# Attention mixed with a Fourier transform on one core: the first score of a full section ahead of the first product, and a value product that waits for the last exponential

## Chip, core and metric

The kernel runs on one core of one Trainium2 chip. The metric is device time of one execution in microseconds, as the median of several runs. Lower is better. The core's engines are named as in the profile: PE multiplies matrices, PEld is its loading of weights, DVE (vector), ACT (scalar), POOL and SP.

## What is computed

Sequence 2048, width 512, 32 heads of 16. Two branches over the same length are mixed by a gate for each row: a Fourier mixing of `A_x` (two transforms by matrix products, real part) and full softmax attention over the same input.

```python
a = jnp.einsum("bsd,ed->bse", x, dft_hid_re)
b = jnp.einsum("bsd,ed->bse", x, dft_hid_im)
y = jnp.einsum("ts,bse->bte", dft_seq_re, a) - jnp.einsum("ts,bse->bte", dft_seq_im, b)
...
qkv = (x @ wqkv)                      # 32 heads, Dh = 16
p = softmax(einsum("bhqd,bhkd->bhqk", q, k) * scale)
o = jnp.einsum("bhqk,bhkd->bhqd", p, v) @ wo
...
g = _sigmoid((x * gate_w).sum(-1, keepdims=True))
return g * a_branch + (1 - g) * b_branch
```

In the reference both branches read `A_x` (`x = A_x`).

## The kernel before

Everything is laid out by hand: the program text gives each engine its order, and PE's order is written as patterns of slots.

Heads are taken in 16 pairs. For a pair, two kinds of score matmul run over the same queries and keys. `a_tile` (L277) makes a tile `a` of 128 queries by 512 keys (matmul at L283), of which DVE takes the row maximum (L285). `scores` (L751) makes a tile `s` of 128 keys by 512 queries (L764), shifted by the maxima found earlier; ACT takes its exponential into a tile `pt` (L765). A head's operands lie in one half of the partitions, 48 or 50 rows, so a score matmul occupies half of the array's rows. `pv` (L778) multiplies the exponentials by the values: four matmuls of 128 by 17 into the four 32-partition strips of one accumulator `acc` (L786), over 16 key tiles; then ACT copies `acc` out (L790). A unit is one key tile of 512 exponentials for each of two query blocks and two heads; `pt` has four buffers.

In the other half of the array's rows, at the same time, run the products of the Fourier transform over the sequence: `dft` (L480) yields them, `Chain.mm` (L446) issues them (L450). An accumulation chain takes 48 products of full depth; each is split into the two halves of the rows, and they are issued in groups of 16, first all 16 in one half, then the same 16 in the other.

`segment` (L889) issues one such half: a section. `pairs` (L921) sends two sections for each group; 192 sections are "full" (`FULL`, L863). A full section has 16 slots and ends with the value products of two units, eight matmuls. In each slot one product `d` is issued with the one half of the rows, and then one score, `s` or `a`, with the other half; the number in a slot is the PSUM bank that the score goes to. Six banks serve the scores, ACT and DVE give them back. The two patterns are:

```python
FULL = "s2 a3 s4 a1 s5 s2 a0 s3 a4 s1 a5 s2 a0 s3 a4 a1 | |", "a5 s2 a1 s0 a4 s3 a5 s2 s0 a1 a3 s4 s2 s5 a0 a1 | |"
```

The second is used in one of eight, where `acc` has just been finished and ACT has it to copy: 24 sections begin with a maximum's score `a`, 168 with an `s`. The bank of slot 0 in the first pattern, 2, is taken again in slots 5 and 11; slot 13's bank, 3, is that of slot 7; slot 15's bank, 1, that of slot 9.

The first product of a section carries a wait, set by hand (L910): when its chain has begun, for the user (exponential or reduction) of the last score that the section before issued after its last product. In the patterns that is the reduction of `a1`. The chain's bank `d` is a single one: a new chain's first product waits until ACT has read the chain before.

Of the kernel before, what the change touches and what calls it, by code (L numbers as in the profile page):

```python
# [22 lines left out]
NT = S // P  # L23
# [8 lines left out]
def mix_kernel(ctx: ExitStack, tc: tile.TileContext, xa_t, xa, wqkv, w_hid, w_seq, wo, gate_w, out):  # L32
# [5 lines left out]
    nc = tc.nc  # L38
# [59 lines left out]
    acc = psO.tile([P, 512], F32, name="acc")  # L98
# [91 lines left out]
    with tc.tile_pool(name="qk", bufs=1, reuse_waits="tile") as pool:  # L190
# [38 lines left out]
        for tb in range(4):  # L229
# [4 lines left out]
            for c in range(2):  # L234
                if tb == 0 and c == 0:
                    pss = [bank() for _ in range(4)]
                    for kt in range(KT):
                        x = xab[tb][:, :, :, kt * P:(kt + 1) * P]
                        for i, (w, v) in enumerate(((wh, 0), (wl, 0), (wh, 1))):
                            for ct in range(4):  # L240
                                nc.tensor.matmul(pss[ct], w[:, c, kt, ct * P:(ct + 1) * P], x[:, :, v],
                                                 start=kt == 0 and i == 0, stop=kt == KT - 1 and i == 2)
# [15 lines left out]
    vt = main.tile([P, NT, NP, 33], F32, name="vt")  # L258
# [18 lines left out]
    def a_tile(i, h, ps=None, bank=None):  # L277
        p, j = divmod(i, 64)
        qt, kb = divmod(j, 4)
        if ps is None:  # L280
            ps = psA.tile([P, 512], F32, "a", bank)
        r = slice(64 * h, 64 * h + 48)
        nc.tensor.matmul(ps, qs[p % 2][r, qt * P:(qt + 1) * P], ks[p % 2][r, kb * 512:(kb + 1) * 512],  # L283
                         start=True, stop=True)
        user = nc.vector.tensor_reduce(mx[p % 2][:, h, qt, kb:kb + 1], ps, AX.X, ALU.max)  # L285
        hf = j // 32
        a_left[p, hf] = a_left.get((p, hf), 64) - 1
        if not a_left[p, hf]:
            deferred.extend((partial(m_parts, p, hf), partial(m_rows, p, hf)))
        return user  # L290
# [460 lines left out]
    def scores(u, qb, h, bank=(psS, "s"), number=None):  # L751
        p, r = divmod(u, 32)
        hf, kt = divmod(r, 16)
        q0 = hf * 1024 + qb * 512
        if u >= UNITS - 16:

            blk, kt = divmod(kt, 8)
            q0, kt = 1024 + blk * 512, 2 * kt + qb
        if u not in pts:
            pts[u] = work.tile([P, 4, 512], F32, name="pt", bufs=4)  # L760
        pool, name = bank
        ps = pool.tile([P, 512], F32, name=name) if number is None else pool.tile([P, 512], F32, name, number)
        rr = slice(64 * h, 64 * h + 50)
        nc.tensor.matmul(ps, ks[p % 2][rr, kt * P:(kt + 1) * P], qs[p % 2][rr, q0:q0 + 512], start=True, stop=True)  # L764
        return nc.scalar.activation(pts[u][:, 2 * qb + h], ps, AF.Exp, bias=0.0, scale=DH ** -0.5)  # L765

    def pv_last(u):
        blk, k2 = divmod(u - UNITS + 16, 8)
        pt = pts.pop(u)
        for j in range(4):  # L770
            x, h = divmod(j, 2)
            nc.tensor.matmul(acc[32 * j:32 * j + 17], vt[:, 2 * k2 + x, NP - 1, 16 * h:16 * h + 17], pt[:, j],  # L772
                             start=k2 == 0, stop=k2 == 7)
        if blk == 0 and k2 == 7:
            last_pairs.append(LastPair(0, [(psS, "s"), (psA, "a")]))
            last_pairs[0].copy(1)

    def pv(u):  # L778
        if u >= UNITS - 16:
            return pv_last(u)  # L780
        p, r = divmod(u, 32)
        hf, kt = divmod(r, 16)
        pt = pts.pop(u)
        for j in range(4):
            h = j % 2
            nc.tensor.matmul(acc[32 * j:32 * j + 17], vt[:, kt, p, 16 * h:16 * h + 17], pt[:, j],  # L786
                             start=kt == 0, stop=kt == NT - 1)
        if kt == NT - 1:
            oe = work.tile([P, 512], F32, name="oe", bufs=2)
            nc.scalar.copy(oe, acc)  # L790
            for qb in range(2):
                nc.sync.dma_start(o_d[hf][p, :, qb * 512:(qb + 1) * 512], oe[64 * qb:64 * qb + 64])

    def take(gen, n, whole=True):

        got = []
        while len(got) < n:
            x = next(gen, None)
            if x is None:
                break  # L800
            x[0].left -= 1
            got.append((*x, x[0].left == 0))
            if whole and got[-1][4]:
                break
        return got

    def issue(x, half, stop=True):
        chain, st, mv, after, last = x
        i = chain.mm(st, mv, half, last and stop)
        if stop and after:  # L810
            after()
        return i
# [15 lines left out]
    for hf in range(2):  # L828
        for ct in range(4):
            n = 3 if hf and ct == 3 else 4  # L830
# [32 lines left out]
    FULL = "s2 a3 s4 a1 s5 s2 a0 s3 a4 s1 a5 s2 a0 s3 a4 a1 | |", "a5 s2 a1 s0 a4 s3 a5 s2 s0 a1 a3 s4 s2 s5 a0 a1 | |"  # L863
# [10 lines left out]

    streams = [stream(h) for h in range(2)]

    users, valued = [], 0

    def score(kind, h, number=None):
        x = next(streams[h][kind == "a"], None)  # L880
        if x:
            users.append((kind, a_tile(*x, bank=number) if kind == "a" else scores(*x, number=number)))

    def values():
        nonlocal valued
        pv(valued)
        valued += 1

    def segment(pattern, half, ds, stop):  # L889


        nonlocal users
        before, users = users, []
        ds = iter(ds)
        for slot in pattern.split():
            number = None
            if slot[1:].isdigit():
                slot, number = slot[0], int(slot[1])
            if slot == "|":
                values()  # L900
                continue
            if len(slot) == 1:
                x = next(ds, None)
                if x:

                    before = before if x[0].begun else None
                    i = issue(x, half, stop)
                    users = []
                    if before:
                        tc.add_manual_dep(  # L910
                            i.ins, dict(before).get("s", before[0][1]).ins.name,
                            mybir.DependencyInfo(mybir.DependencyClass.Sync, mybir.DependencyReason.DATA))
                        before = None
            if slot != "-":
                score(slot[-1] if slot[0] == "+" else slot[0], 1 - half, number)
            if len(slot) == 2 and slot[0] != "+":
                score(slot[1].lower(), half)
        if deferred:
            deferred.pop(0)()
# [17 lines left out]
    pump(hid, 12)  # L937
    ds = take(hid, 12)
    segment(START[0], 0, ds, False)
    pump(hid, 12)  # L940
    segment(START[1], 1, ds, True)
    values()
    values()
    for patterns, ds in pairs():
        for half in range(2):
            run_plan(valued)
            pattern = FULL[valued % 16 == 0] if patterns is FULL else patterns[half]
            segment(pattern, half, ds, half == 1)
# [14 lines left out]
    for u in range(valued + 2, UNITS, 2):  # L963
# [12 lines left out]
        values()  # L976
    last_pairs[0].products([(psS, "s"), (psA, "a"), (psA, "a"), (psD, "d")], range(4))
    pv(UNITS - 2)
    pv(UNITS - 1)
    last_pair(late)  # L980

# [35 lines left out]
```

## Time and profile before

| | |
|---|---|
| median of 3 runs | 1703.69 us (1703.32 to 1705.98) |
| the profiled execution, in all | 1703.4 us |
| its span | 1701.6 us |
| PE busy | 1693.8 us, 13040 matmuls |
| PE's weight loads busy | 1053.0 us |
| DVE busy | 1352.7 us |
| ACT busy | 1152.2 us |
| POOL busy | 449.7 us |
| granted TensorE clock | 1.0 |
| HBM traffic | 107.73 MB read, 54.52 MB written |

The profile is one execution. A row of the groups names the line of the kernel, the engine, the operation, output and input tiles, shapes and count, then busy time and mean duration, and behind the second bar the idle time just before and what ended it. A row of the timeline has its start and its duration in microseconds, then engine, line and operation; a count above one means that neighbouring rows of one kind were drawn together, from the first one's start to the last one's end. PEld is a load of weights, PE the matmul that uses them. What stands in brackets is the engine's idle time before and the engine and tile that ended it. Matmuls are pipelined and their ends are modelled: a matmul of 512 columns is shown with some 0.39 us, though the next of the same half starts 0.23 us later.

### The profile page before, as it was taken

The page shows a single profiled execution, that of the slowest core. Times are in us where ns is not written, and L with a number is a line of the kernel's source. Part 1 is how long each engine was busy: PE and PEld are TensorE (multiplying, and loading weights), DVE is VectorE, ACT ScalarE, POOL GpSimd, SP SyncE. Part 2 cuts the span into 40 slices and gives each one's busy share as a digit, 9 for nine tenths or more (in the row PEclk, how much of TensorE's full clock was granted, in tenths as well). Part 3 has the DMA queues.
Part 4 walks back from the last instruction along what each step waited for, and adds up shares of the span by engine and source line. Part 5 has one row for each costly group of instructions (what it writes and reads, how often), then busy time and mean ns, then how long its engine had stood idle before and what let it go on. Part 6 is the DMA issues. An engine that isn't in the chain of part 4 may idle for free.

```text
span 1701.6 us, 33689 instructions
## 1 busy us (share of the span) xinstructions
PE 1693.8 (100%) x13040; PEld 1053.0 (62%) x13040; DVE 1352.7 (79%) x2289; ACT 1152.2 (68%) x2266; POOL 449.7 (26%) x554
## 2 busy tenths in 40 slices
PE   9999999999999999999999999999999999999998
PEld 7888755556666666666666666666666666655444
DVE  5439888888888888888888888888888888889854
ACT  5212377777767777667777777776677777678886
POOL 0101121322222333222222343322323343211110
PEclk9999999999999999999999999999999999999999
DMA  9963500314141434314146435224141535352114
GB/s 294 346 144 136 154 8 17 42 38 76 57 77 45 88 97 99 71 39 82 38 94 243 96 107 109 67 60 79 46 86 57 122 106 102 131 183 42 32 34 138
DMA packets 82130, 165.10 MB, mean 97 GB/s; under 512 B 19444, under 2 KB 19682, under 8 KB 78130
## 3 DMA queue, kind: packets, MB, share of 16 engines
q1 hardware_dynamic: 77874, 162.12, 37.1%
q8 instruction: 103, 1.69, 0.4%
q0 software_dynamic: 3808, 0.30, 0.2%
q14 instruction: 57, 0.47, 0.1%
q10 hardware_dynamic: 288, 0.52, 0.1%
HBM read 107.73 MB, written 54.52 MB: 95 GB/s over the span
## 4 chain that ended last, share of the span: by engine, by line
PE 99%; DMA 0%; DVE 0%; ACT 0%; DVEq 0%; issue 0%
PE d L450 37%; PE acc L786 27%; PE a L283 12%; PE s L764 10%; PE s L364 3%; PE s L396 1%; PE d L364 1%; PE acc L772 1%; PE a L107 1%; PE a L106 1%; PE s L107 1%; PE s L106 1%; PE a L105 1%; PE s L105 1%; PE s L450 1%; PE a L450 0%
## 5 line engine op out<-in xcount | busy, mean ns | idle before, releaser
L285 DVE TENSOR_REDUCE mx<-a 128x1 f32<-128x512 f32 x2026 | 1241.0, 682 | 242.6 <-PE a L283 212.8
L765 ACT ACTIVATE pt<-s 128x512 f32<-128x512 f32 x2006 | 1022.6, 620 | 359.4 <-PE s L764 289.9
L764 PE MATMUL s<-qs,ks 50*128 50x512 f32 x2006 | 787.0, 422 | 0.0
L283 PE MATMUL a<-ks,qs 48*128 48x512 f32 x2026 | 744.3, 400 | 0.0
L450 PE MATMUL d<-xab,ch 64*128 64x512 f32 x2016 | 648.0, 396 | 0.0
L786 PE MATMUL acc<-pt,vt 128*17 128x512 f32 x3968 | 484.1, 596 | 0.0
L450 PEld LDWEIGHTS d<-xab,ch 64*128 64x128 f32 x2016 | 365.1, 184 | 124.2 <-DVE mx L285 60.4
L764 PEld LDWEIGHTS s<-qs,ks 50*128 50x128 f32 x2006 | 365.0, 185 | 68.9 <-issue 16.8
L283 PEld LDWEIGHTS a<-ks,qs 48*128 48x128 f32 x2026 | 369.4, 186 | 60.1 <-DVE mx L285 23.9
L450 PE MATMUL d<-xab,cl 64*128 64x512 f32 x1008 | 399.3, 396 | 0.0
L450 PEld LDWEIGHTS d<-xab,cl 64*128 64x128 f32 x1008 | 185.5, 184 | 63.7 <-DVE mx L285 40.8
L434 POOL CAST ch<-craw 128x512 fp32r<-128x512 f32 x126 | 77.2, 612 | 551.2 <-PE a L283 214.2
L786 PEld LDWEIGHTS acc<-pt,vt 128*17 128x17 f32 x3968 | 86.0, 96 | 201.3 <-issue 201.3
L435 POOL TENSOR_TENSOR cl<-craw,ch 128x512 fp32r<-128x512 f32 x126 | 162.1, 1287 | 10.2
L308 POOL DMA_DIRECT2D qs<-mt x119 | 67.0, 568 | 157.7 <-DVE mt L302 155.2
L450 PE MATMUL d<-wre,xab 64*128 64x512 f32 x336 | 90.4, 402 | 0.0
L450 PEld LDWEIGHTS d<-wre,xab 64*128 64x128 f32 x336 | 59.0, 184 | 38.6 <-issue 23.3
L450 PE MATMUL d<-wo_hl,o_hl 64*128 64x512 f32 (+1 forms) x246 | 68.2, 409 | 0.0
L450 PEld LDWEIGHTS d<-wo_hl,o_hl 64*128 64x128 f32 (+1 forms) x246 | 42.2, 184 | 29.3 <-issue 12.2
L101 ACT CAST hl<-s 128x512 fp32r<-128x512 f32 x28 | 16.2, 588 | 58.4 <-PE d L364 25.1
L468 POOL CAST xab<-y 128x512 fp32r<-128x512 f32 x16 | 9.8, 611 | 127.7 <-ACT y L466 99.6
L637 POOL TENSOR_TENSOR yp<-yp,few 128x512 f32<-128x512 f32 x12 | 15.4, 1281 | 105.3 <-ACT few L636 105.2
(167 smaller groups left out, 1000.5 us busy)
## 6 DMA issues: line engine op xcount, KB each, us to landing
craw<-w_seq SPq DMA_DIRECT2D x128, 256.0 KB
qk<-hl SPq DMA_DIRECT2D x32, 512.0 KB
qs<-qk SPq DMA_DIRECT2D x96, 128.0 KB
ks<-qk SPq DMA_DIRECT2D x96, 128.0 KB
b<-hl SPq DMA_DIRECT2D x16, 512.0 KB
xab<-b SPq DMA_DIRECT2D x16, 512.0 KB
o<-oe SPq DMA_DIRECT2D x62, 128.0 KB
oh<-nh SPq DMA_DIRECT2D x12, 512.0 KB
```

Of the source, the lines that this page charges most:

```text
L105: nc.tensor.matmul(ps, sh, mh, start=first, stop=False)
L106: nc.tensor.matmul(ps, sh, ml, start=False, stop=False)
L283: nc.tensor.matmul(ps, qs[p % 2][r, qt * P:(qt + 1) * P], ks[p % 2][r, kb * 512:(kb + 1) * 512], start=True, stop=True)
L285: user = nc.vector.tensor_reduce(mx[p % 2][:, h, qt, kb:kb + 1], ps, AX.X, ALU.max)
L308: (nc.gpsimd if own else nc.sync).dma_start(rows.rearrange("v (q b c) -> v b q c", q=8, b=4)[:, b], mt[hf][32 * b + h:32 * b + 32:2])
L364: i = nc.tensor.matmul(ps, st[r], mv[r], start=not half and not j, stop=half == 1 and j == 11)
L434: nc.gpsimd.tensor_copy(h1, raw)
L435: nc.gpsimd.tensor_tensor(l1, raw, h1.bitcast(F32), ALU.subtract)
L450: i = nc.tensor.matmul(self.ps, st[r], mv[r], start=not self.begun, stop=stop)
L764: nc.tensor.matmul(ps, ks[p % 2][rr, kt * P:(kt + 1) * P], qs[p % 2][rr, q0:q0 + 512], start=True, stop=True)
L765: return nc.scalar.activation(pts[u][:, 2 * qb + h], ps, AF.Exp, bias=0.0, scale=DH ** -0.5)
L786: nc.tensor.matmul(acc[32 * j:32 * j + 17], vt[:, kt, p, 16 * h:16 * h + 17], pt[:, j], start=kt == 0, stop=kt == NT - 1)
```

## The change

Three things, all in the issuing of full sections. `pv` and `values` return the last matmul of the value products, and `score` keeps the latest exponential. At the end of a full section the last matmul of the second unit's value products gets a dependency on the section's last exponential (that of slot 13). And in slot 0 of a pattern whose slots are numbered, which only the full patterns are, the score is issued ahead of the product; in the other slots the product stays ahead. So PE's order at the section's start is score, product, product, score, product, score, where it was product, score, product, score. The product's own wait is kept.

```diff
@@ pv
-            nc.tensor.matmul(acc[32 * j:32 * j + 17], vt[:, kt, p, 16 * h:16 * h + 17], pt[:, j],
-                             start=kt == 0, stop=kt == NT - 1)
+            i = nc.tensor.matmul(acc[32 * j:32 * j + 17], vt[:, kt, p, 16 * h:16 * h + 17], pt[:, j],
+                                 start=kt == 0, stop=kt == NT - 1)
...
+        return i
@@ score, values
-    users, valued = [], 0
+    users, valued, exponential = [], 0, None
...
+            if kind == "s":
+                exponential = users[-1][1]
...
-        pv(valued)
+        i = pv(valued)
         valued += 1
+        return i
@@ segment
-        for slot in pattern.split():
+        for n, slot in enumerate(pattern.split()):
...
             if slot == "|":
-                values()
+                i = values()
+                if n == len(pattern.split()) - 1 and pattern in FULL:
+                    tc.add_manual_dep(i.ins, exponential.ins.name,
+                                      mybir.DependencyInfo(mybir.DependencyClass.Sync, mybir.DependencyReason.DATA))
                 continue
+            if not n and number is not None:
+                score(slot, 1 - half, number)
             if len(slot) == 1:
                 x = next(ds, None)
...
-            if slot != "-":
+            if slot != "-" and (n or number is None):
                 score(slot[-1] if slot[0] == "+" else slot[0], 1 - half, number)
```

DVE's, ACT's, POOL's and SP's instructions and their order are the same in both programs; on PE the 192 first scores move by one place. Which instruction of PE announces its end to the other engines is settled when the program is built: an instruction's count is carried by the next one behind it, so long as that one waits for nothing.

More of the change, by code (lines that the diff above doesn't have):

```diff
@@ L875, in mix_kernel @@
     streams = [stream(h) for h in range(2)]
-    users, valued = [], 0
+    users, valued, exponential = [], 0, None
     def score(kind, h, number=None):
+        nonlocal exponential
         x = next(streams[h][kind == "a"], None)
```

## The prediction

> **What bounds the kernel now.** I read the page first: PE is busy throughout, and the chain that ended last stays on it.
>
> ```profile
> span 1701.6 us, 33689 instructions
> PE d L450 37%; PE acc L786 27%; PE a L283 12%; PE s L764 10%; PE s L364 3%; PE s L396 1%; PE d L364 1%; PE acc L772 1%; PE a L107 1%; PE a L106 1%; PE s L107 1%; PE s L106 1%; PE a L105 1%; PE s L105 1%; PE s L450 1%; PE a L450 0%
> L285 DVE TENSOR_REDUCE mx<-a 128x1 f32<-128x512 f32 x2026 | 1241.0, 682 | 242.6 <-PE a L283 212.8
> L765 ACT ACTIVATE pt<-s 128x512 f32<-128x512 f32 x2006 | 1022.6, 620 | 359.4 <-PE s L764 289.9
> L786 PE MATMUL acc<-pt,vt 128*17 128x512 f32 x3968 | 484.1, 596 | 0.0
> ```
>
> A busy PE hides waits inside its matmuls, so I went to the timeline of one full section, in order of time (start, duration). Times below are differences of starts.
>
> ```profile
> 598.12 1.04 PE L786 MATMUL acc<-pt,vt 128*17 128x512 f32 x8
> ...
> 599.09 0.18 PEld L450 LDWEIGHTS d<-xab,cl 64*128 64x128 f32 x1 [0.85 <-DVE mx L285]
> 599.10 0.50 PE L450 MATMUL d<-xab,cl 64*128 64x512 f32 x1
> ...
> 599.10 0.49 PE L764 MATMUL s<-qs,ks 50*128 50x512 f32 x1
> ...
> 599.43 0.39 PE L450 MATMUL d<-xab,ch 64*128 64x512 f32 x1
> ...
> 599.66 0.60 ACT L765 ACTIVATE pt<-s 128x512 f32<-128x512 f32 x1 [1.91 <-PE s L764]
> ...
> 600.31 0.18 PEld L764 LDWEIGHTS s<-qs,ks 50*128 50x128 f32 x1
> ...
> 601.59 1.12 ACT L765 ACTIVATE pt<-s 128x512 f32<-128x512 f32 x2
> ...
> 602.66 0.39 PE L450 MATMUL d<-xab,cl 64*128 64x512 f32 x1
> 602.76 0.18 PEld L283 LDWEIGHTS a<-ks,qs 48*128 48x128 f32 x1
> ...
> 602.84 0.42 PE L283 MATMUL a<-ks,qs 48*128 48x512 f32 x1
> 603.18 0.62 PE L786 MATMUL acc<-pt,vt 128*17 128x512 f32 x4
> ```
>
> The reader is to see a loop through ACT. The value products' block ends at 599.16 (598.12 + 1.04); product and first score start at 599.10. The first exponential starts 0.56 after that score and ends at 600.26; slot 5's score, which takes the first one's bank, loads weights at 600.31, 0.05 later. The same 0.05 stands at the end: the sixth exponential (the second of the pair from 601.59) ends at 602.71, slot 15's score loads at 602.76, and the value products start 0.42 after that load. Between first and sixth exponential ACT runs back to back. So in the usual section the time from first score to value products is: 0.56 to the first exponential, about 3.05 of six exponentials, 0.05 + 0.42. That is 4.08, and it moves one for one with the start of the **first exponential**. The products are ahead by then: the last one starts at 602.66, the last score at 602.84, so their stream has 0.18 of slack. DVE has some too, as shown below.
>
> **The order at the section's start.** The change puts the first score in front of the first product. Neither waits for the other; both wait for the end of the value products. What changes is the announcing. In the programs as built, 136 of the 168 sections that begin with a score have, before, a product with a semaphore increment of its own, and the score's increment behind it. In 32 sections (31 first products of a new accumulation chain, and the first section of all) the product has none, its count being added to the score's. These 32 are what the changed kernel does everywhere: there the score comes first, its increment carries the value products' eight (nine in all), and the first products' counts go with the next score's. Here is one such section, the one after that shown above:
>
> ```profile
> 605.02 0.18 PEld L450 LDWEIGHTS d<-xab,ch 64*128 64x128 f32 x1 [0.85 <-POOL cl L435]
> ...
> 605.03 0.49 PE L764 MATMUL s<-qs,ks 50*128 50x512 f32 x1
> ...
> 605.57 4.03 ACT L765 ACTIVATE pt<-s 128x512 f32<-128x512 f32 x8 [1.31 <-PE s L764]
> ...
> 609.09 0.62 PE L786 MATMUL acc<-pt,vt 128*17 128x512 f32 x4
> ```
>
> Score to exponential takes 0.54, and score to value products 4.06 where the neighbour took 4.08. First and last of the 136 (361.79 and 1488.67), then first and last of the 32 (355.54 and 1459.01), each with the exponential, and for the two last ones the value products:
>
> ```profile
> 361.79 0.49 PE L764 MATMUL s<-qs,ks 50*128 50x512 f32 x1
> ...
> 362.36 0.60 ACT L765 ACTIVATE pt<-s 128x512 f32<-128x512 f32 x1 [1.90 <-PE s L764]
> ...
> 1488.67 0.50 PE L764 MATMUL s<-qs,ks 50*128 50x512 f32 x1
> ...
> 1489.23 0.60 ACT L765 ACTIVATE pt<-s 128x512 f32<-128x512 f32 x1 [1.90 <-PE s L764]
> ...
> 1492.75 0.62 PE L786 MATMUL acc<-pt,vt 128*17 128x512 f32 x4
> ...
> 355.54 0.50 PE L764 MATMUL s<-qs,ks 50*128 50x512 f32 x1
> ...
> 356.08 0.60 ACT L765 ACTIVATE pt<-s 128x512 f32<-128x512 f32 x1 [0.53 <-PE s L764]
> ...
> 1459.01 0.50 PE L764 MATMUL s<-qs,ks 50*128 50x512 f32 x1
> ...
> 1459.55 0.60 ACT L765 ACTIVATE pt<-s 128x512 f32<-128x512 f32 x1 [1.32 <-PE s L764]
> ...
> 1463.07 0.62 PE L786 MATMUL acc<-pt,vt 128*17 128x512 f32 x4
> ```
>
> 0.57 and 0.56 against 0.54 and 0.54; 4.08 against 4.06. Rows are rounded to 0.01; in the unrounded records the medians are 0.564 over the 136 and 0.538 over the 32, and 4.088 and 4.060 to the value products. **Step 1:** 136 x 0.026 = 3.5 us less (bounds from the rounded rows: 0.02 to 0.03, 2.7 to 4.1). The Trainium skill, "TensorE: Matmul & The Clock Gate", section "The cost: per-tile semaphore tail", says that completion increments go one after another and gives 26.3 ns for each; by it the step is 136 x 0.0263 = 3.6 us, an estimate the rows bear out.
>
> **Step 2:** the score takes the product's place, one place ahead: 599.09 against 599.10 for their starts, 0.003 unrounded. In all 168 sections that is 0.5 us (bounds 0 and 168 x 0.01 = 1.7; the rows' difference is rounding, so I take the unrounded one). The product falls back by as much, under its slack of 0.18: product and score run in different halves of the array. In the other 24 sections a maximum's score goes first and the exponentials are set by slot 1, whose place doesn't change: 0.
>
> **The product's wait** for the last reduction stays; one score is now ahead of it instead of behind.
>
> ```profile
> 599.89 4.88 DVE L285 TENSOR_REDUCE mx<-a 128x1 f32<-128x512 f32 x8 [1.05 <-PE a L283]
> ```
>
> Its eight reductions end at 604.77, 0.25 before the next section's first load at 605.02, though the page names DVE as releaser of such loads. So this wait ends early, and putting a score over it is worth 0; it would cost if reductions came 0.25 later.
>
> **The value products' new wait.** The last product of the block now waits for the section's last exponential. Queued behind it on PE are the first score and product of the next section. The rows of a usual section, then of one of the 24 sections with the other pattern (their eighth exponential against the value products):
>
> ```profile
> 603.02 0.67 ACT L765 ACTIVATE pt<-s 128x512 f32<-128x512 f32 x1
> ...
> 603.63 1.04 PE L786 MATMUL acc<-pt,vt 128*17 128x512 f32 x8
> ...
> 626.91 0.62 PE L786 MATMUL acc<-pt,vt 128*17 128x512 f32 x4
> 626.97 0.66 ACT L765 ACTIVATE pt<-s 128x512 f32<-128x512 f32 x1
> ...
> 627.35 1.04 PE L786 MATMUL acc<-pt,vt 128*17 128x512 f32 x8
> ```
>
> The exponential ends at 603.69; with the 0.05 of wake-up the load goes at 603.74. The waiting product itself starts at 604.08 (603.63 + 1.04 less one matmul of 0.59), so 0.34 is left. With the other pattern: 627.63 + 0.05 = 627.68 against 628.39 - 0.59 = 627.80, 0.12 left. Price 0 (bounds 0 and the slower rival's price). If the cover were gone, each section would pay what the exponential lacks.
>
> What the wait buys is that the next first score carries none. What a score without a wait does behind value products is shown in the last stage, where some blocks already end in a waiting product and a score without a wait follows:
>
> ```profile
> 1529.98 1.05 PE L786 MATMUL acc<-pt,vt 128*17 128x512 f32 x8
> ...
> 1530.96 0.19 PEld L764 LDWEIGHTS s<-qs,ks 50*128 50x128 f32 x2 [0.85 <-issue]
> 1530.96 0.50 PE L764 MATMUL s<-qs,ks 50*128 50x512 f32 x2
> ```
>
> Its load goes 0.07 before the block's end (1531.03), as with a wait (599.09 against 599.16), and the block takes 1.05 as one without a wait does (1.04). Price 0 both ways. Late announcement of the value products (with the score, some 0.5 later) meets nobody: the next exponentials wait for that score anyway, and where ACT copies the accumulator the block keeps its own increment. Queues of SP, POOL, ACT and DVE are unchanged.
>
> **Sum:** 3.5 + 0.5 = 4.0 us. Against the profiled execution, 1701.6 of span and 1703.4 in all, that is 1699.4; the median of 1703.69 is 0.3 above that execution, so **1699.7**. Own range of this case: 2.7 + 0.5 to 4.1 + 0.5, that is 1699.1 to 1700.5.
>
> **Rivals.** *Nothing but the order (13 in 100):* the 0.026 of the 32 sections belongs to the new chain, not to the increment, or another wait takes it back. For it: DVE, with more busy time than ACT (1241.0 against 1022.6), gives half of the banks back. Against it: the 4.06, where the gain arrives whole. Then 0.5 is left: 1703.2.
>
> *The load goes under the value products (6):* without a wait, the first score's weights are loaded early. Its matmul takes 0.49 where one with a hidden load takes 0.39: 0.10 x 168 = 17 us more, 1683. Against it the rows at 1530.96. The Trainium skill, the same page, section "Step-by-step: what each phase is for", says that loads are pulled ahead of running matmuls if the row groups don't conflict or the load goes to the background buffer; by the second clause this rival would hold, by the first it can't, since value products use all rows, and the trace sides with the first.
>
> *The new wait becomes the bound (11), slower:* the place is the fourth strip of the block's last product. Now its load goes with the running pass, about 603.63; with the wait at 603.74, and with the other pattern 0.33 later (627.68 against 627.35). If the array's strips can't start apart, the whole block is late by that: 168 x 0.11 + 24 x 0.33 = 26 us, less 4.0: 1726. It decides as soon as a late load isn't hidden behind the running pass, or, with hiding, once exponentials end 0.34 (0.12) later. Against it: the 1.05 block, though there the wait may have been met long before.
>
> **How the numbers follow.** The main case gets 70. Told apart from no change is what exceeds 0.2%, 3.4 us: below 1700.3 or above 1707.1. Of the 70, 54 lie below 1700.3 (its range reaches 1700.5 only at its slow end) and 16 within. Faster 54 + 6 = 0.60; same 16 + 13 = 0.29; slower 0.11. Range 1698.2 to 1704.3: main case and the rival without gain with some scatter of the runs (1703.32 to 1705.98); out are the 6 and the 11.
>
> **What would show it.** Right: in all 168 sections the first exponential 0.54 after the first score and 4.06 from there to the value products; slot 5 and slot 15 still 0.05 behind an exponential. Step 2: the score's load first, still 0.07 before the block's end. The wait: blocks of 1.04 with four matmuls starting together. Wrong: a first exponential still at 0.56; the fourth strip starting apart; a section's gain lost in a later wait for DVE; a first score of 0.39.

## The result, and the profile after

The changed kernel takes 1699.24 us (median of 9 runs, 1698.87 to 1700.21) beside 1703.6 us before (9 runs, 1703.24 to 1705.98): 4.4 us less, a ratio of 0.9975 with a 95% interval of 0.9966 to 0.9983. The profiled execution took 1700.21 us in all, the slowest of the nine; its span is 1698.4 us, against 1701.6 us before.

The page of the changed kernel: the rows that answer to those shown before, and two on weight loads:

```profile
span 1698.4 us, 33689 instructions
L285 DVE TENSOR_REDUCE mx<-a 128x1 f32<-128x512 f32 x2026 | 1240.9, 683 | 238.4 <-PE a L283 215.5
L765 ACT ACTIVATE pt<-s 128x512 f32<-128x512 f32 x2006 | 1023.0, 619 | 354.0 <-PE s L764 335.6
L764 PEld LDWEIGHTS s<-qs,ks 50*128 50x128 f32 x2006 | 364.6, 185 | 207.8 <-issue 158.8
L786 PE MATMUL acc<-pt,vt 128*17 128x512 f32 x3968 | 484.1, 596 | 0.0
L450 PEld LDWEIGHTS d<-xab,ch 64*128 64x128 f32 x2016 | 366.2, 184 | 20.6
```

The two rows on weight loads as they were before:

```profile
L450 PEld LDWEIGHTS d<-xab,ch 64*128 64x128 f32 x2016 | 365.1, 184 | 124.2 <-DVE mx L285 60.4
L764 PEld LDWEIGHTS s<-qs,ks 50*128 50x128 f32 x2006 | 365.0, 185 | 68.9 <-issue 16.8
```

Work is the same: in these rows counts, mean durations and busy times stand as before, within 1.1 us. What has moved is idle time. ACT waited 359.4 us in front of exponentials and now waits 354.0. The idle time in front of a section's first weight load stood with the product, most of it put down to DVE; now it stands with the score as "issue", 158.8 us in 188 places (16.8 in 21 before), some 0.85 us each, as long as before. So that time never was a wait for DVE: the value products run in it.

The section that answers to the one shown before (timeline; start and duration in us), from its value products to the next ones:

```profile
597.51 1.48 PE L786 MATMUL acc<-pt,vt 128*17 128x512 f32 x12
...
598.81 0.61 PE L786 MATMUL acc<-pt,vt 128*17 128x512 f32 x4
599.35 0.18 PEld L764 LDWEIGHTS s<-qs,ks 50*128 50x128 f32 x1 [0.85 <-issue]
599.35 0.49 PE L764 MATMUL s<-qs,ks 50*128 50x512 f32 x1
...
599.35 0.49 PE L450 MATMUL d<-xab,cl 64*128 64x512 f32 x1
...
599.88 0.60 ACT L765 ACTIVATE pt<-s 128x512 f32<-128x512 f32 x1 [1.87 <-PE s L764]
...
600.12 0.69 DVE L285 TENSOR_REDUCE mx<-a 128x1 f32<-128x512 f32 x1 [1.02 <-PE a L283]
...
600.53 0.18 PEld L764 LDWEIGHTS s<-qs,ks 50*128 50x128 f32 x1
...
601.83 1.11 ACT L765 ACTIVATE pt<-s 128x512 f32<-128x512 f32 x2
...
602.99 0.18 PEld L283 LDWEIGHTS a<-ks,qs 48*128 48x128 f32 x1
...
603.41 0.62 PE L786 MATMUL acc<-pt,vt 128*17 128x512 f32 x4
```

The score's load goes first, at 599.35, and still 0.07 before the end of the value products (598.81 + 0.61 = 599.42). The first exponential follows its score by 0.53, where it was 0.56. The two places where PE waits for ACT are unchanged: slot 5 loads at 600.53, 0.05 behind the first exponential's end (600.48); slot 15 loads at 602.99, 0.05 behind the sixth's (602.94). From score to value products it is 4.06. In the unrounded records, as medians over the kinds of section:

| | sections | first exponential behind the score | score to value products | period |
|---|---|---|---|---|
| before, product announced ahead of the score | 136 | 0.564 | 4.088 | 5.934 |
| before, product not announced | 32 | 0.538 | 4.060 | 5.904 |
| after, score first (without two single ones: the first section, and one product that still announces itself) | 166 | 0.534 | 4.061 | 5.903 |
| before, second pattern | 24 | | | 5.945 |
| after, second pattern | 24 | | | 5.939 |

136 x 0.031 + 32 x 0.001 + 24 x 0.006 = 4.4 us, which is as much as the median of the runs moved. The spans of the two profiled executions differ by 3.2 only, because the one after took 1.3 longer ahead of the sections: the value products just before the first one began at 355.81, before at 354.55 (in the traces of the first four experiments below, at 354.46 to 355.28). From there to the value products of the last section it is 4.5 shorter, 1133.7 against 1138.2.

The new wait, a little later in the same timeline, where the last strip's load is the one that waits:

```profile
603.26 0.65 ACT L765 ACTIVATE pt<-s 128x512 f32<-128x512 f32 x1
603.41 1.48 PE L786 MATMUL acc<-pt,vt 128*17 128x512 f32 x12
...
603.86 0.21 PEld L786 LDWEIGHTS acc<-pt,vt 128*17 128x17 f32 x4 [0.31 <-issue]
604.29 0.12 PEld L786 LDWEIGHTS acc<-pt,vt 128*17 128x17 f32 x4 [0.22 <-issue]
```

The exponential ends at 603.91. The four loads of the second unit take 0.21 from first start to last end, where four unhindered ones take 0.12 (the row at 604.29): the last of them goes about 0.1 late, at 603.96, as the wake-up of 0.05 makes it. The block doesn't feel it: its matmuls run on.

### The profile page after: what moved, and what is told of

The parts are those of the page before. It is cut to its first block, busy times and chain, and to the rows that moved or that the text cites. A ratio compares the mean times of both kernels' runs of the same rounds, so it can differ in the third digit from the quotient of the medians.

```text
span 1698.4 us, 33689 instructions
## 1 busy us (share of the span) xinstructions
PE 1689.8 (99%) x13040; PEld 1067.1 (63%) x13040; DVE 1352.6 (80%) x2289; ACT 1152.6 (68%) x2266; POOL 450.5 (27%) x554
## 4 chain that ended last, share of the span: by engine, by line
PE 99%; DMA 0%; DVE 0%; DVEq 0%; ACT 0%; SPq 0%; issue 0%
PE d L450 32%; PE acc L786 27%; PE s L764 14%; PE a L283 13%; PE s L364 3%; PE s L396 1%; PE d L364 1%; PE acc L772 1%; PE a L107 1%; PE a L105 1%; PE s L107 1%; PE s L105 1%; PE a L106 1%; PE s L106 1%; PE s L450 1%; PE a L450 0%
## 5 line engine op out<-in xcount | busy, mean ns | idle before, releaser
L765 ACT ACTIVATE pt<-s 128x512 f32<-128x512 f32 x2006 | 1023.0, 619 | 354.0 <-PE s L764 335.6
L764 PEld LDWEIGHTS s<-qs,ks 50*128 50x128 f32 x2006 | 364.6, 185 | 207.8 <-issue 158.8
L786 PEld LDWEIGHTS acc<-pt,vt 128*17 128x17 f32 x3968 | 102.2, 96 | 185.2 <-issue 179.6
```

What stands on the lines that cost most here:

```text
L786: i = nc.tensor.matmul(acc[32 * j:32 * j + 17], vt[:, kt, p, 16 * h:16 * h + 17], pt[:, j], start=kt == 0, stop=kt == NT - 1)
```

## The experiments

Each is the changed kernel, as it is or with one part altered. The first four ran on one chip in 5 rounds, beside the same runs of the kernel before: 1704.33 us (20 runs, 1703.32 to 1706.47).

### The changed kernel again

> The changed kernel again, beside the parts of it on the same chip. 1699.2 us as before, within 0.7; first exponential 0.534 behind the first score and sections of 5.90 in its profile.

1700.2 us (8 runs, 1699.59 to 1700.86), ratio 0.9972 (0.9962 to 0.9983). On this chip both kernels are slower than in the result above, by 0.7 and 1.0 us, so the time expected is missed by 0.3; the ratio is the same within its interval. The times expected for the next three leave out this shift too. In the profile the first exponential is 0.535 behind its score and the period is 5.908.

### The order alone

```diff
                 i = values()
-                if n == len(pattern.split()) - 1 and pattern in FULL:
-                    tc.add_manual_dep(i.ins, exponential.ins.name, ...)
```

> The order alone: the first score ahead of the first product, no added wait. Theory of the announcement (the first exponential comes 0.026 to 0.030 earlier because no increment of another matmul goes just before the score's): the score carries its own wait and its own increment again, but it is first, so the whole gain stays: first exponential 0.53 to 0.54 behind the score, 1699.3 us (1698.7 to 1700.2). Rival, that it is the wait taken off the first score that pays: first exponential at 0.56, gain only from the place, 0.5 us, 1703.1.

1700.21 us (7 runs, 1699.78 to 1700.47), ratio 0.9973 (0.9962 to 0.9983): the same as the changed kernel on this chip, so the whole gain without the added wait. The timeline of the same section:

```profile
598.98 0.18 PEld L764 LDWEIGHTS s<-qs,ks 50*128 50x128 f32 x1 [0.85 <-issue]
598.98 0.50 PE L764 MATMUL s<-qs,ks 50*128 50x512 f32 x1
...
599.51 0.60 ACT L765 ACTIVATE pt<-s 128x512 f32<-128x512 f32 x1 [1.88 <-PE s L764]
...
599.78 0.69 DVE L285 TENSOR_REDUCE mx<-a 128x1 f32<-128x512 f32 x1 [1.03 <-PE a L283]
...
603.05 0.62 PE L786 MATMUL acc<-pt,vt 128*17 128x512 f32 x4
```

Exponential 0.53 behind the score, value products 4.07 behind it, although here the score carries a wait and an increment of its own. So what pays is not the wait that the score lost. The row of DVE adds something: with this order the score of slot 1 is announced behind a product's increment again, and its reduction starts 0.80 behind the section's score, against 0.77 in the changed kernel (1.325 and 1.300 behind the last value product's start in the unrounded medians). The section is no longer for it, so DVE has slack of at least that.

### The wait alone

```diff
-            if not n and number is not None:
-                score(slot, 1 - half, number)
...
-            if slot != "-" and (n or number is None):
+            if slot != "-":
```

> The wait alone: the last value product waits for the last exponential, the product stays ahead of the first score. Theory of the announcement: the score carries no wait any more, so the product's count goes with the score's and no increment stands before it: first exponential 0.538 behind the score as in the 32 sections of before, 136 x 0.026 = 3.5 us, 1700.1 us (1699.5 to 1700.8). Rival, that the score's place is what pays: no gain, 1703.6; rival, that the added wait costs: over 1703.6.

1701.23 us (10 runs, 1700.62 to 1701.58), ratio 0.998 (0.997 to 0.9989): 3.1 us less than before, 1.0 us more than with the order. The time lies 0.4 above the range expected, which counted from 1703.6; the gain of 3.1 is 0.4 under the 3.5 expected. The product is ahead again, but no longer announces itself:

```profile
598.69 0.49 PE L450 MATMUL d<-xab,cl 64*128 64x512 f32 x1
598.69 0.18 PEld L764 LDWEIGHTS s<-qs,ks 50*128 50x128 f32 x1
598.69 0.49 PE L764 MATMUL s<-qs,ks 50*128 50x512 f32 x1
...
599.23 0.60 ACT L765 ACTIVATE pt<-s 128x512 f32<-128x512 f32 x1 [1.87 <-PE s L764]
...
602.76 0.62 PE L786 MATMUL acc<-pt,vt 128*17 128x512 f32 x4
```

0.54 and 4.07; unrounded, the exponential is 0.538 behind its score as the median of 167 sections, what the 32 sections of before showed. The one section in which the product still announces itself ahead of the score has 0.566. Where such a product stands behind the score, in one section of the changed kernel and two of the order alone, it is 0.532 and 0.536. So each part of the change brings most of the gain alone, and they don't add up: either way no product's increment goes ahead of the score's. That is what this kernel, the one with the order alone, and the 32 sections of before have in common at that place, against the 136.

### The wait on the first product of the second unit

```diff
-            i = nc.tensor.matmul(acc[32 * j:32 * j + 17], vt[:, kt, p, 16 * h:16 * h + 17], pt[:, j], ...)
+            x = nc.tensor.matmul(acc[32 * j:32 * j + 17], vt[:, kt, p, 16 * h:16 * h + 17], pt[:, j], ...)
+            i = i if j else x
```

> The changed kernel with the wait on the first instead of the last product of the second unit. The load of that product would go 0.55 behind the block's start, with 0.3 left until it starts: theory of the cover: 1699.2 us as the changed kernel. Rival, that a late load holds up the three strips behind it or breaks the four apart: at least 0.1 a section, 192 x 0.1 = 19 us, 1718 or more.

1699.85 us (6 runs, 1699.68 to 1700.61), ratio 0.9971 (0.996 to 0.9983): no dearer than the changed kernel. Its timeline:

```profile
596.31 1.48 PE L786 MATMUL acc<-pt,vt 128*17 128x512 f32 x12
596.86 0.11 PEld L786 LDWEIGHTS acc<-pt,vt 128*17 128x17 f32 x4 [0.42 <-ACT pt L765]
...
598.16 0.18 PEld L764 LDWEIGHTS s<-qs,ks 50*128 50x128 f32 x1 [0.85 <-issue]
```

Here all four loads wait, and ACT ends their wait 0.55 behind the block's start, 0.1 later than they would go. The next section's load comes 1.85 behind the block's start, as in the changed kernel within rounding (599.35 - 597.51 = 1.84; unrounded 1.840 in both). This late load too is hidden behind the running pass.

### The wait on the last product of the first unit, where nothing covers it

```diff
-                if n == len(pattern.split()) - 1 and pattern in FULL:
+                if n == len(pattern.split()) - 2 and pattern in FULL:
```

> The changed kernel with the wait on the last product of the first unit, where nothing covers it: that product normally starts 0.02 behind the block's start, and the exponential ends 0.50 behind it (0.73 with the second pattern). Theory of the cover: each section pays what the exponential lacks and the wake-up, 168 x 0.53 + 24 x 0.76 = 107 us, 1806 us (1790 to 1815); the profile shows the fourth strip starting alone. Rival, that the wait ends early here too or the block has slack: 1699.2.

1806.93 us (2 runs, 1806.67 to 1807.19), ratio 1.0604 (1.0574 to 1.0635), beside 1703.1 us before on its chip: 108 us more than the changed kernel's 1699.24 of the result above, where 107 had been worked out.

```profile
617.96 1.14 ACT L765 ACTIVATE pt<-s 128x512 f32<-128x512 f32 x2
...
618.59 2.45 PE L786 MATMUL acc<-pt,vt 128*17 128x512 f32 x16
619.15 0.11 PEld L786 LDWEIGHTS acc<-pt,vt 128*17 128x17 f32 x5 [0.43 <-ACT pt L765]
...
620.97 0.18 PEld L764 LDWEIGHTS s<-qs,ks 50*128 50x128 f32 x1 [0.85 <-issue]
```

The exponential ends at 619.10, the waiting load goes at 619.15, and the block ends at 621.04 (618.59 + 2.45), 0.53 later than usual. In the unrounded records of this block the matmuls of three strips start at 0.00 to 0.01, 0.44 to 0.46, 0.87 to 0.88 and 1.30 to 1.31 behind its start, as in the changed kernel; those of the fourth at 0.56, 1.00, 1.43 and 1.86. The next section's load comes 2.38 behind the block's start instead of 1.84. The price of the wait, once uncovered, is what the exponential lacks: the change would have paid it, had it put the wait one unit earlier.

### The first two slots exchanged

```diff
-    FULL = "s2 a3 s4 a1 s5 s2 a0 s3 a4 s1 a5 s2 a0 s3 a4 a1 | |", ...
+    FULL = "a3 s2 s4 a1 s5 s2 a0 s3 a4 s1 a5 s2 a0 s3 a4 a1 | |", ...
```

> The changed kernel with the first two slots of the first pattern exchanged (a3 s2 instead of s2 a3): the first exponential comes 0.24 later (its score starts 0.34 later but with its weights loaded behind another matmul, 0.39 instead of 0.49), DVE's first reduction as much earlier. Theory of ACT's loop (score to value products moves one for one with the first exponential): 168 x 0.24 = 41 us, 1740 us (1730 to 1750). Rival, that the banks of both engines together set the pace: 10 us at most, 1699 to 1709. Rival, that DVE's reductions set it: faster than 1699.

1739.65 us (2 runs, 1739.4 to 1739.9), ratio 1.021 (1.018 to 1.0239). The rows begin with the section's first score, now one for DVE:

```profile
607.42 0.50 PE L283 MATMUL a<-ks,qs 48*128 48x512 f32 x1
...
607.76 0.39 PE L764 MATMUL s<-qs,ks 50*128 50x512 f32 x1
...
607.96 0.69 DVE L285 TENSOR_REDUCE mx<-a 128x1 f32<-128x512 f32 x1 [0.81 <-PE a L283]
...
608.20 0.60 ACT L765 ACTIVATE pt<-s 128x512 f32<-128x512 f32 x1 [2.12 <-PE s L764]
...
611.72 0.62 PE L786 MATMUL acc<-pt,vt 128*17 128x512 f32 x4
```

First exponential 0.78 behind the section's start, value products 4.30: both 0.24 more than in the changed kernel (0.53 and 4.06; unrounded 0.243 and 0.239), while DVE's first reduction starts 0.23 earlier (0.54 against 0.77). One for one with ACT, and nothing from DVE: the loop that the prediction drew sets the length of these 168 sections, and the rival of the banks of both engines, at most 1709 us, is out.

## Why the prediction was right

**The bound.** That the length of a section which begins with a score hangs on its first exponential is what the forecast rests on, and the exchange of slots shows it over 0.24 us a section, eight times the change's effect. That was a delay; the other way it holds as far as the next wait. In 46 of the 168 sections (23 of the 136, 23 of the 32) the third and the fourth product carry increments of their own. There the changed kernel's third exponential starts 1.530 behind the first score, in the other 122 sections 1.507, and the value products come at 4.066 instead of 4.059. The first exponential is as early in both. By the order of the increments it is the same effect again, before the third score; no run has these increments taken away.

**Step 1, the announcing.** Forecast 0.026 in each of 136 sections, 3.5 us. The wait alone, which leaves PE's order as it was, gave 3.1 us on the clock and 0.538 in the profile. Right in place, and in size within 0.4. What lies behind it was read from two groups of sections of one trace; the two part kernels make the rivals (a new chain, the lost wait) fall, since each shows the gain without the one or the other. That increments go one after another in the hardware is a reading of it and isn't shown further.

**Step 2, the place.** Forecast 0.003 a section, 0.5 us; order and wait against wait alone is 1.0 us (1701.23 against 1700.2). This term was mis-sized: besides the 0.003 of the earlier load, the exponential follows its score by 0.534 instead of 0.538 when the score is ahead, 0.007 together. It also falls on other sections than forecast. Summed over the traces of the two part kernels, the order's advantage is 0.91 us in the 136 sections (0.007 each), 0.02 in the 32, and 0.21 in the 24 of the second pattern, 1.1 us in all. In the 32, most of which are among the 46 above, the first exponential is as much earlier and the section is not shorter. In the sum the difference hardly shows: 4.0 forecast, 4.4 measured, 1699.24 against 1699.7. That is in part luck: of the two steps measured apart, the first came out 0.4 under its forecast and the second 0.5 over.

**The second pattern** was put at 0, because its exponentials keep their place. Its 24 sections are 0.006 shorter, 0.1 us in all, although the first exponential starts 0.003 later behind the last value product (1.325 against 1.322). What is earlier there is DVE's first reduction, by 0.007 (1.058 against 1.065), and the load of the last score goes 0.053 behind the end of a reduction, where the first pattern's goes 0.051 behind the end of an exponential. So these sections hang on DVE, which the prediction didn't see.

**The product's wait for DVE** was put at 0, and the load at the section's start goes at the same distance from the value products in all seven kernels, whoever stands first and with or without a wait (0.52 behind the start of the last matmul). So the first score doesn't come under the value products, as the rival of 1683 had it (its matmul still takes 0.49), and the first product starts 0.003 later by standing behind it, well under its slack.

**The value products' new wait** was put at 0 with 0.34 and 0.12 of cover. It does make a load late, in every section, and it is hidden, on the first strip as on the last; where the cover is taken away it costs what was worked out. The slower rival had a real mechanism and the wrong place.

## What to carry to other kernels

Look in a busy engine's timeline for the loop that goes through another engine, and find the one instruction that starts it: here 0.03 us at the first exponential was worth 0.03 us in each of 136 sections, while DVE's first reduction could move by 0.23 us for nothing. An instruction that a consumer is waiting for should be the first to announce itself: products that stand ahead of it are better left without an increment of their own. Issuing it first was enough here; a wait that is put on an earlier, covered instruction is another way, since it lets counts be carried together, and added nothing to the order. After such a change look for the next wait of the loop, here the third score's. Before adding a wait, work out its cover: the same wait cost nothing on the second unit's products and 108 us on the first unit's last.

## What was not expected

The four strips of a value product keep their own time: with the fourth held back by 0.54 us, the other three ran through all their passes as usual and only the block's end moved. The slower rival had taken it for possible that they can't start apart. And a matmul that finishes with another and is issued ahead of it, without announcing anything, still seems to delay the other's consumer by some 4 ns (0.538 against 0.534), which 168 sections make just visible; why stays open.
